# Key buffers zeroed in part by ScalarE, one-product key eviction, DMA transposes for two token blocks: a two-layer attention and mixer kernel

## The chip, the cores and the metric

The kernel runs on one core of a Trainium2 chip. A core has five engines that work at the same time, each through its own list of instructions: TensorE (PE; matrix products, results in PSUM), VectorE (DVE), ScalarE (ACT; activation functions), GpSimd (POOL) and SyncE (SP), from which this kernel issues its DMA transfers. Engines wait for each other through semaphores. The metric is the device time of one execution in microseconds (us). Before the change the median of three runs is 436.9 us (435.96 to 437.09).

## What is computed

Two layers, each an attention block A with a sliding window of 256 tokens (32 heads of 16 columns) and a mixer block B that works across tokens. There are 2048 tokens of 512 columns, in bfloat16; the same weights serve both layers. Both blocks normalise their input twice, once in the line that calls them (block B again inside).

```python
def _A_ref(x, wqkv, wo):
    B, S, D = x.shape
    H = 32; Dh = D // H; W = 256
    qkv = (x @ wqkv).reshape(B, S, 3, H, Dh).transpose(2, 0, 3, 1, 4)
    q, k, v = qkv[0], qkv[1], qkv[2]
    scores = jnp.einsum("bhqd,bhkd->bhqk", q, k) * (Dh ** -0.5)
    idx = jnp.arange(S)
    mask = (idx[:, None] - idx[None, :] >= 0) & (idx[:, None] - idx[None, :] < W)
    scores = jnp.where(mask[None, None], scores, -1e9)
    p = _softmax(scores, axis=-1)
    o = jnp.einsum("bhqk,bhkd->bhqd", p, v)
    return o.transpose(0, 2, 1, 3).reshape(B, S, D) @ wo

def _B_ref(x, w1, b1, w2, b2):
    h = _layernorm(x, axis=-1)
    u = _gelu(jnp.einsum("bsd,sf->bdf", h, w1) + b1)
    y = jnp.einsum("bdf,fs->bds", u, w2) + b2
    return y.transpose(0, 2, 1)

x = x + _A_ref(_layernorm(x, axis=-1), A_wqkv, A_wo)
x = x + _B_ref(_layernorm(x, axis=-1), B_w1, B_b1, B_w2, B_b2)
x = x + _A_ref(_layernorm(x, axis=-1), A_wqkv, A_wo)
x = x + _B_ref(_layernorm(x, axis=-1), B_w1, B_b1, B_w2, B_b2)
```

## The kernel before

**Tiling.** Tokens are cut into 16 blocks of 128 (`x_sb[:, t]`, normalised in `xh_sb[:, t]`) and into four quarters of four blocks (`m` = 0 to 3). Head columns are cut into four groups of 128 (`o` = 0 to 3), eight heads each. `prepare(m)` makes queries, keys and values of a quarter; `attention` then takes chunks of 64-token pieces (in layer 0 four or eight pieces, in layer 1 eight).

**A quarter** (`qkv`). Each block is normalised: statistics (L471, L473) on VectorE, the reciprocal root on POOL (L484), subtract and multiply on VectorE (L491). It is then transposed into `xhT`, either by TensorE against an identity (L549) with a copy out of PSUM on VectorE or ScalarE (L556, L558), or by a DMA transpose issued by SP (L542). Before the change all four blocks of quarter 0 in layer 0 go by TensorE and every other block by DMA. Quarter 0 of layer 0 is worked in two halves (columns 0 to 255, then 256 to 511), in the code the loop over `a, b` with `first` true for the first half. All matrix products of projections, the output product and the mixer's first parts go through `mm_group` (L513).

**Keys.** Scores are computed with two heads stacked in a row group of 32, so keys are kept in `kbd` with each head's columns spread to its own half and zeros in the other. In quarter 0 most keys are evicted from PSUM straight into `kbd`, by two operations that multiply with the columns of the 0/1 table `par` (L582 on ScalarE, L583 on VectorE). Other keys go through a staging tile `stg` (L594, L596) and from there by one of three ways: eight DMA copies of the rows that hold data (L604, which need the zeros written before), or two multiplications with `par` on POOL or VectorE (L609, which write the zeros too). Two memsets on POOL (L461) zero slots 1 and 2 of `kbd` at the start.

**Values.** Each pair of blocks is evicted into `vst` (L631, L633) and spread by four DMA copies into `vb` (L636).

**Attention.** Scores (L690) fill two pairs of PSUM banks; ScalarE computes the exponential into `pt` (L705); POOL or VectorE masks the diagonal pieces (L726) with the integer constants `ldm` and `ldn`, which are made at the start from a triangle `tri` on POOL (L430, L431) and six VectorE operations (L433, L435, three of L439, L454). Products with values (L747) follow, then a transpose, a reciprocal and a product (L767, L771, L773) and a second transpose (L778). Products of the next quarter and of the mixer fill TensorE's time between scores.

**The order.** Every operation is recorded as an `op` with what it reads and writes, and many with alternatives (`alts`: the same work on another engine). `ORDER` is a packed text that holds, for each place of the whole program, which operation comes next and which alternative it takes; `replay` gives each engine its list from it, and `emit` writes the semaphore waits. Each engine works in the order of its list. SP's DMAs stand in such a list too: a transfer that waits holds the ones behind it.

At the start TensorE runs 36 products on a block of ones (L392, `f_warm`), ScalarE loads its table of functions (L916), and SP issues the loads of x (L401) and of the weights (L405).

Of the kernel before, what the change touches and what calls it, by code (L numbers as in the profile page):

```python
# [7 lines left out]
dt = mybir.dt  # L8
# [7 lines left out]
    'c-qBQJ&5a87Cw^iym#m24ro9DE$D$>P@zHr1r$&~4;*kn0Tl{p!G#}q!G!|~IH1A-2lN&PwBQ9TIN-tyE*x;-!V50EV3sLdcwrV?xbVUhQ@EI7Sf+5{!o?nq'  # L16
    '$20ciz5Hx8yJyB%_g-CH-SeIAd`ALMAW$=FmRTW@UM>_MC=^Pi;EO_mPE}Ps8;@00Q*G-bFh2xcf8YPD^Jy4{4r?wJVNeNZF(i;5j)u<AALc&kTb8BtuoYXD'
    'EV9&YSZ!4!>!g`bN{ewkFV?-!CZqniE{d#Ft%9xV!b#)(TCEaPYV5=_a)q2Md&JD;Y}-<ZEX(4%qNtz|nGh-nqM(nNFd2`>41lrbFj=oV>y08w5=@sO5l;Q9'
    'E5~t`4k7c4g`?**4MwApcs`k)PYEH@>2%p2_m%ug%J;zU^<}w}Bmj_HTwbUu%%gUDrPRKHF)ZpZ8V-j>IkgT#q9zGxwOWL+*Q6H5QAD5FVugcBIS8UCVtAx5'
    'oJ<&u19$iv7cna1#_*YKJ5^OyJ|z~OtkC_q)3F@aao}aY-|XcJja+V-4ePd#=6Nr5$8=54^GwtKgfnf&d1+c%n=zA#x^CzI129br?M|l+Elo!hRD}YZf_Qqu'  # L20
    'SP)3ERD?p|W-T+p<AlWmmz&J>+$%~ixu#_`=S`xiFBAY-2B_6)1cnJql2x_3URO7ptD9B5K6*wd)Vkd{-aVgQFQ<Q>cFUdVVsW`#OsA3K%;)o&*{hi55Q9-J'
    '&$FfBG&||^{?_aDDLp%bAP7veKNy<kcP63}C9PHz{n0aH$ElgsxDhjE)LBq-b-g0Gt{ca(`sEk$b^TQ&DrE65;-xkz7100?E&w~1%|a*V<m_xVrnDCQ9!bX-'
    'm1YXX*h}M)fU!Om&@okIOl(PvC5<{j12J|S3bq}Tigu~!`;_{gMNNZdeg7q;j;bwzsGwS!B?u~0Ziq%Y!^?{V8oI8Zce{fD0`^>Em^H0dLzbj46plFn<Ww=A'
    'FQK`4LOj>DNP1RH&t|jQXq06s1sG+39kbi*t^uyE!Cc~!i-kgzrhK_Xo{tGG>%nMzHqPfML1rY`Bx!fr#C02P^EJAFZ(cjutY58xXXjs)hPF-A3lBL3pX4lJ'
    'o4RQ@9~cBgQ$#}$1OcwgE@B2$AdHBjArra3DN3SFkg5WD1k-axgz>l%2E(u)1b&%$CBINMT;FsZMb~r1oPiq~IYiJfbj!AeLw#WAgbe9`w0dBuuGqvgRI6$j'
    'Lc4<2z`#YeO+!o3Fn0_>IzT9qQcL7U7do+6@7L?yx^*Vrn%pXe80Su@MFqwhm|>=H;=0V37#a(!ArlQI2rlNJAe`WqOfhG#%;{=H-5W~sx^x5=7q*a+gflh$'
    'eZw$Pt#TZr6a%Qw`y4VQmouyne9JOS0EC7qvVzDPj44PKNl{G8B<pp1eIlAyme0J)%S%H$)eL|an)+N(`aLv4B*F~_HO#v|s2W6@$RDsi$nbjkB_tw<aCUYk'
    '2%!wcfUen!F_|78BN06ngymAB$TM;-Nt5|()|t)vvzaWn&qvv;Tm`7MhvtWaKA@`N30<K-=(ly9A_Jd|R8$)In<f)_y+1(=bS0n$TwlMwx<cq7j=u@(C`omM'
    's+WpyhcVx0`At5b6!LM*{CvrmDw0$xmkNc#rysW*%d#2dEs#FcKqmsA;wpwx&^1K`SfV3>fB;P<6ID1nqf~>FlQsVIBw?qUO$1{_QR7&{n2;j^pNrDz@KvRP'
    'TuK<mIr4oZ1y_!9SyUwYJ76btI<*!T3yU5b?QZw{9Hy=d9K2`0HxPs}^t#>t;Lp8&uVtQFrU}$Q`lqt{ZNl~Yf`ICa&~-Y75XsujO{=A87$B%rB7GV}b(9zY'  # L30
    '!{`(WoNg6MMP0AzkT0PA69N(@pXYm16Wzfq^z*(fYqEw}a{7X?cLkw<Ig%y~Rv3X&ok}t$2N6%!f^;N~$NkaC$qf0x1Uyf>-6bt(Dr%$g90?}?KF5_9Bjq&r'
    '9VRfOm7H#+>+RW`V$C>FkB<j`i7}q|K(_<XYPW`Ah;7)b*Etl+sQ&d=xDeCKb@TZ=swXnG*RcqAC>3m#2FEZ|10}nJyGwXDa!fJMLOcUE@4D;t8rCTF_KdDp'
    '|1^yA<<&pVaphmfWICUu<!>~UB*XY_G#-s?$tqjlN}AScVXSKL*K!D9S_VJ=yjH4~LRu`AgEE#cl(BpvpVe)WwLK4sNQCSM`bXp=iwJ^1G+BAkm!89|;E<#0'
    '5m!-^W`k?os-6+90>f~bsiaDi{tQqkm1!RJ6VNdN6KJ;<Xrpm^*cw#FsDIU@*6DORRU@vZyI^4JQ7JM?MU+}7R=i5t^UGK(hjfISwCi<9P;1@T^KGmPwx6?$'
    '*`}Si72oo#we1*=ty>Z<K|oE*NRs|kQo3VFj-qBWDr2RP%}Py=YhYMbK*X6DDpU<N!bV@P(lwST5xh&(i+Q7GS|c{pKw4GeK!HfSMw)Ln+D&j%-rOMigkF)W'
    'tIbAOU&8!+J`XM&6!y_r8jXS!q*_hOK?T1v(t@EBna)rd<f<%4h$aS4NQ;jOl%l*~OW_w9_o&0&&v3hj+gnZ!duhI<*Czn)Jlx^9hb0`)bV%+FN`XV$Zku+n'
    '%>ZN|?LN&sO}kq=zHOhv-X((zp6<=U-J8*Pa_H5QU5DrIHq7vcHy#^*d!K)d4tMK5e>l${9Ua~EIN<K_y7Py7!t>njX^wjX)W6uc-L~877SOvn4xM=XCjR#3'
    'ffxM4i0An?kYc;%9Wwk|$-{APJ07>ksr#_L-FWzK8n-+D0aDygj{&!b@9tr^=Pk!^+<%y7KZ6b2k1gcj|6*(}X#Cwjf54*cklzn(I)3MF&FvFM_fPP5OiFd)'
    'PDWB$dFT6#-?q>0yM*KRNS1zT!}g1NyGbT<D<hdyr!twhb1?I;1+K~*&h7>o9{)0XkL(?vf4BgDKjPoOZ+@F@{L_OaPq}pBkzPEK;jMa+EjG7q-XVq8Cxq-~'
    'fqY-CA5M)9kj(yDwjO2Pn4mw1SmuWW<UnaM{7ypdNwS?t+e|9Z`@ub6^$)5i|0od;xd4x4`DbU#p|J1k!A{$`U5U8saSyKSuRIv-&+SBsdzd5tlMLqG#I842'  # L40
    'njg9Q>mP6%x*dvl<9p-|jZg3K-1a{$!)bv|s~^WdEIxed;iHG!)%)G|$*<zszX32A5e)'
# [211 lines left out]
def mm_cost(n, cols):  # L253
    return n * (cols / 2.4 + 4.0)
# [50 lines left out]
def bass_interleave_layers__sliding_block__mixer_token_mlp__prompt_kernel(  # L305
# [29 lines left out]
    with es:  # L335
# [86 lines left out]
        for h in range(2):  # L422
# [10 lines left out]
        op("vector", lambda e: e.tensor_scalar(ldm[:, 0, :], tri[:, 0:64], half[:, 0:1], 0.0, op0=ALU.mult, op1=ALU.add),  # L433
           reads=["tri"] + HALF, writes=["ld0"])
        op("vector", lambda e: e.scalar_tensor_tensor(ldm[:, 0, :], tri[:, 64:128], half[:, 1:2], ldm[:, 0, :],  # L435
                                                      op0=ALU.mult, op1=ALU.add), reads=["tri", "ld0"] + HALF,
           writes=["ld0"])
        for i, m, c in ((1, 1.0, 0.0), (2, -1.0, 1.0), (3, -1.0, 1.0)):
            op("vector", lambda e, i=i, m=m, c=c: e.tensor_scalar(ldm[:, i, :], ldm[:, 0, :], m, c, op0=ALU.mult, op1=ALU.add),  # L439
               reads=["ld0"], writes=[f"ld{i}"])  # L440
        LD = [f"ld{i}" for i in range(4)]
# [18 lines left out]
        for k in (1, 2):  # L460
            op("gpsimd:zero", lambda e, k=k: e.memset(kbd[:, k].rearrange("p a b c d -> p (a b c d)").bitcast(dt.float32), 0.0),  # L461
               writes=["kz0"], cost=1900)
# [56 lines left out]
        def mm_group(kind, dst, n, mk, reads, cols=512, step=2, prio=None, holds=(), after=()):  # L519

            prio = fprio() if prio is None else prio
            for k0 in range(0, n, step):
                k1 = min(n, k0 + step)

                def f(e, cols32, k0=k0, k1=k1):
                    last = None
                    for k in range(k0, k1):
                        last = matmul(e, cols32, *mk(k), start=(k == 0), stop=(k == n - 1))
                    return last
                rd = reads(k0, k1) if callable(reads) else reads  # L530
                op("tensor:" + kind, f, reads=rd, writes=[dst], cost=mm_cost(k1 - k0, cols), prio=prio, holds=holds, after=after, cfg="f",
                   cls="f", flex=True)


        def qkv(m, before, split, layer):
# [3 lines left out]
            def transpose(i, wide):  # L539
# [7 lines left out]
                def f_tr(e):  # L547
# [4 lines left out]
                op("tensor:ftr", f_tr, reads=[f"xh{t}", "ident"], writes=[ft], cost=4 * 60, prio=fprio(),  # L552
                   holds=[tx], cfg="f", cls="f")
# [6 lines left out]
            def proj(o, which, a, b, wide):  # L560
# [3 lines left out]
                at = lambda: bank(ft)[:, 0:n]  # L564
                staged = m > 0 or (not layer and (o, a) in STAGED)
# [11 lines left out]
                if not staged:  # L577
                    src = lambda: at().rearrange("p (s n) -> p s n", n=64)

                    def f_ka(e, act=False):  # L580
                        for h in range(2):
                            last = (e.activation(dst(h), src(), ACTF.Copy, scale=par[:, h:h + 1]) if act else  # L582
                                    e.tensor_scalar(dst(h), src(), par[:, h:h + 1], 0.0, op0=ALU.mult, op1=ALU.add))  # L583
# [14 lines left out]
                def f_kz(e):  # L598
                    got = []
                    assert layer or m > 2 or tk.slot  # L600
# [6 lines left out]
                def f_kz2(e):  # L607
                    for h in range(2):
# [34 lines left out]
            for a, b in ((0, 256), (256, 512)) if split else ((0, 512),):  # L643
# [4 lines left out]
                for i in range(a // P, b // P):  # L648
                    transpose(i, first if m == 0 and not layer else None)
# [339 lines left out]
```

## Time and profile before

| | |
|---|---|
| median of three runs | 436.9 us |
| the profiled execution | 436.27 us |
| its span in the trace | 434.5 us |
| TensorE busy | 420.9 us (97%) |
| VectorE busy | 322.6 us (74%) |
| ScalarE busy | 317.0 us (73%) |
| POOL busy | 187.2 us (43%) |
| granted TensorE clock | 1.00 in every stretch |
| first exp (L705) | 9.40 us |
| TensorE busy in 0 to 40 us | 33.7 of 40 us |

The span is the time from the first to the last event of the trace; the device time has 1.8 us more around it. "Busy" counts an engine's instructions; matmuls are pipelined, so a TensorE that is busy throughout need not be at its peak. In the page's slices each digit is the busy share of 10.9 us in tenths. The chain of waits is followed back from the last instruction: at each step it goes to what released the waiting instruction. A line such as "L705 ACT" names the line of the kernel's text and the engine.

### The profile page before, as it was taken

Reading aid. Unit: us, or ns where it says so; the run is one execution under the profiler, and the core shown is the slowest. Engines: PE = TensorE matmul, PEld = TensorE weight load, DVE = VectorE, ACT = ScalarE, POOL = GpSimd, SP = SyncE. Lnnn points to the kernel's source line nnn. Section 1 sums busy time; section 2 is a strip of 40 time slices with the busy share of each in tenths; the row PEclk is TensorE's granted clock in tenths of the full one; section 3 lists DMA queues with packets and bytes.
Section 4 is the critical chain, followed back from the end, with each engine's and each line's share of the span. In section 5 each row is a group of like instructions: output and inputs, shape, how many; then the busy total and the mean of one; then the engine's idle time right before and its main releaser. Section 6 shows DMA issues by size and latency. Waiting matters only on the chain.

```text
span 434.5 us, 14318 instructions
## 1 busy us (share of the span) xinstructions
PE 420.9 (97%) x6177; PEld 188.5 (43%) x6177; DVE 322.6 (74%) x629; ACT 317.0 (73%) x364; POOL 187.2 (43%) x277
## 2 busy tenths in 40 slices
PE   7979989999999999999999999999999999999997
PEld 6534333434444444444444444444434444445443
DVE  7998989779996678556777999989788758422205
ACT  5999999999997953606999999899999870520000
POOL 7788865864664620011465554365435221000000
PEclk9999999999999999999999999999999999999999
DMA  8565262302163257723542282240223262747713
GB/s 237 167 125 88 63 127 37 79 5 49 26 166 83 75 152 211 208 62 88 137 110 52 64 147 64 51 77 11 47 64 99 66 175 69 226 140 213 228 32 115
DMA packets 101850, 46.03 MB, mean 106 GB/s; under 512 B 32156, under 2 KB 101788, under 8 KB 101788
## 3 DMA queue, kind: packets, MB, share of 16 engines
q1 hardware_dynamic: 101788, 45.13, 41.7%
q8 instruction: 49, 0.80, 0.8%
q14 instruction: 13, 0.11, 0.1%
HBM read 33.56 MB, written 2.10 MB: 82 GB/s over the span
## 4 chain that ended last, share of the span: by engine, by line
PE 73%; ACT 18%; DVE 6%; DMA 1%; POOL 1%; issue 0%; SPq 0%
PE PS L513 50%; ACT pt L705 17%; PE PS L868 8%; PE PS L690 8%; PE PS L747 7%; DVE stats L471 1%; DMA vb<-vst 1%; DVE xh_sb L491 1%; DVE pt L726 1%; DVE rl L767 1%; DMA x_sb<-in_A_x_dram 1%; POOL pt L726 0%; DVE stg L594 0%; DVE vst L631 0%; SPq L636 0%
## 5 line engine op out<-in xcount | busy, mean ns | idle before, releaser
L705 ACT ACTIVATE pt<-PS 128x1024 bf16<-128x1024 f32 (+1 forms) x304 | 281.0, 1036 | 13.1 <-PE PS L690 11.9
L726 POOL TENSOR_TENSOR pt<-pt,ldm 128x256 int32<-128x256 int32 (+2 forms) x189 | 125.9, 686 | 101.7 <-ACT pt L705 101.1
L513 PE MATMUL PS<-xhT,wqkv 128*128 128x512 bf16 (+1 forms) x288 | 67.8, 357 | 2.7 <-ACT pt L705 1.9
L513 PE MATMUL PS<-xh_sb,w1b 128*128 128x512 bf16 x280 | 69.9, 381 | 0.1
L513 PE MATMUL PS<-uT,w2b 128*128 128x512 bf16 (+2 forms) x308 | 68.3, 360 | 0.0
L690 PE MATMUL PS<-qT,kbd 32*128 32x64 bf16 (+4 forms) x1552 | 60.2, 247 | 3.1 <-ACT pt L705 2.1
L484 POOL TENSOR_TENSOR rstd<-agg,mhalf 128x2 f32<-128x2 f32 (+1 forms) x33 | 23.8, 722 | 66.8 <-DVE agg L473 66.7
L909 DVE SCALAR_TENSOR_TENSOR x_sb<-PS,bcol,x_sb 128x512 bf16<-128x512 f32 x31 | 22.6, 746 | 38.0 <-PE PS L513 37.7
L690 PEld LDWEIGHTS PS<-qT,kbd 32*128 32x128 bf16 x1552 | 22.7, 92 | 61.7 <-ACT pt L705 45.6
L767 DVE STREAM_TRANSPOSE rl<-PS 128x1024 f32<-128x1024 f32 x32 | 39.9, 1248 | 12.3 <-PE PS L747 12.1
L747 PE MATMUL PS<-pt,vb 64*17 64x128 bf16 (+4 forms) x3104 | 43.6, 248 | 2.4 <-DMA vb<-vst 1.1
L471 DVE BATCH_NORM_STATS2 stats<-x_sb 128x6 f32<-128x512 bf16 x64 | 44.2, 693 | 1.5 <-DMA x_sb<-in_A_x_dram 0.8
L883 ACT ACTIVATE uT<-rl,bcol 128x512 bf16<-128x512 f32 x28 | 18.3, 712 | 33.8 <-DVE rl L879 33.8
L513 PEld LDWEIGHTS PS<-uT,w2b 128*128 128x128 bf16 x308 | 27.5, 98 | 31.1 <-issue 3.2
L747 PEld LDWEIGHTS PS<-pt,vb 64*17 64x17 bf16 x3104 | 31.8, 84 | 17.6 <-issue 7.9
L513 PE MATMUL PS<-uT,pt 128*128 128x512 bf16 x168 | 39.2, 379 | 0.0
L868 PE MATMUL PS<-xh_sb,w1b 128*128 128x512 bf16 x168 | 37.7, 379 | 0.0
L513 PEld LDWEIGHTS PS<-xhT,wqkv 128*128 128x128 bf16 x288 | 24.2, 97 | 30.1 <-issue 6.3
L513 PEld LDWEIGHTS PS<-xh_sb,w1b 128*128 128x128 bf16 x280 | 23.7, 98 | 30.8 <-issue 5.9
L513 PE MATMUL PS<-wqkv,xhT 128*128 128x512 bf16 x128 | 34.2, 381 | 0.2 <-DVE stg L594 0.2
L726 DVE TENSOR_TENSOR pt<-pt,ldn 128x256 int32<-128x256 int32 (+1 forms) x77 | 29.6, 404 | 5.3 <-ACT pt L705 5.0
L513 PE MATMUL PS<-wo_sb,oT 128*128 128x512 bf16 x128 | 32.4, 380 | 0.5 <-ACT pt L705 0.5
(62 smaller groups left out, 340.7 us busy)
## 6 DMA issues: line engine op xcount, KB each, us to landing
w1b<-in_B_w_dram SPq DMA_DIRECT2D x112, 128.0 KB, 2.8
w2b<-in_B_w_dram SPq DMA_DIRECT2D x70, 128.0 KB, 2.8
pt<-in_B_w_dram SPq DMA_DIRECT2D x42, 128.0 KB, 3.0
vb<-vst SPq DMA_DIRECT2D x64, 68.0 KB, 2.1
out_dram<-x_sb SPq DMA_DIRECT2D x15, 128.0 KB, 1.8
x_sb<-in_A_x_dram SPq DMA_DIRECT2D x3, 512.0 KB, 6.2
kbd<-stg SPq DMA_DIRECT2D x80, 16.0 KB, 1.9
wqkv<-in_A_wqkv_dram SPq DMA_DIRECT2D x4, 256.0 KB, 5.4
```

What stands on the lines that cost most here:

```text
L471: op("vector:stat", lambda e: e.bn_stats(st[:, 0:6], x_sb[:, t, :]), reads=[f"x{t}"], writes=[("st", i)], cost=dve_cost(512))
L484: op("gpsimd:rstd", lambda e: e.tensor_tensor(rstd[:, t0:t1, 0], agg[:, t0:t1, 1], mhalf[:, 0:1].to_broadcast([P, t1 - t0]), op=ALU.pow), ...
L491: op("vector:xh", lambda e: e.tensor_scalar(xh_sb[:, t, :], x_sb[:, t, :], agg[:, t, 0:1], rstd[:, t, :], op0=ALU.subtract, op1=ALU.mult), ...
L513: return e.matmul(o, lhsT=w, rhs=x, start=start, stop=stop, skip_group_check=True)
L690: last = e.matmul(bank(tt[r // 2], r % 2)[:, base + c0 * 64:base + (c0 + n) * 64], lhsT=kbd[32 * r:32 * r + 32, tk.slot, o, jj].rearrange( ...
L705: op("scalar:exp", lambda e, ts=ts, tp=tp, i=i, cols=cols: e.activation(probs(tp)[:, i, 0:cols, :], pair(ts)[:, :, 0:cols].rearrange("p r ...
L726: return e.tensor_tensor(v, v, m, op=by)
L747: last = e.matmul(bank(t, h)[32 * r:32 * r + 17, i + q0 * 64:i + (q0 + n) * 64], lhsT=vb[64 * h:64 * h + 64, tk.slot, jj, 4 * o + r, :], r ...
L767: op("vector:od", lambda e, t=tod, tr=tr: e.transpose(rl[:, tr.slot:tr.slot + 2].rearrange("p a b -> p (a b)"), pair(t)), reads=[(tod, i) ...
L868: last = e.matmul(bank(tu, tt), lhsT=v()[:, sc - b0, k0 + tt * P:k0 + (tt + 1) * P], rhs=xh_sb[:, sc, :], start=(sc == b0), stop=(sc == NT ...
L883: op("scalar:gelu", lambda e, ft=ft, tt=tt: e.activation(uT[:, ft, :], rl[:, tmps[tt].slot], ACTF.Gelu_apprx_tanh, bias=b1col[:, ft:ft + 1 ...
L909: op("vector:resy", lambda e: e.scalar_tensor_tensor(x_sb[:, t, :], bank(ft), b2col[:, t:t + 1], x_sb[:, t, :], op0=ALU.add, op1=ALU.add), ...
```

## The change

- The two POOL memsets of `kbd` slots 1 and 2 (128x2048 each) become three of 128x1024 (slot 1, groups 2 and 3; slot 2, groups 0 and 1; slot 2, groups 2 and 3). Each may also be done by ScalarE, as an activation that copies a column of the identity with the scale 0. They come after the load of ScalarE's table, which is recorded earlier in layer 0. Keys of quarter 1, groups 0 and 1, lose the DMA way; only the keys that may go by DMA read the zeros.
- Five VectorE operations for `ldm` become three, of which two may go to POOL; with `ldn` that makes four.
- VectorE's direct key eviction becomes one product that reads the PSUM columns twice, against both columns of `par`. ScalarE's stays as it was.
- Blocks 2 and 3 of quarter 0 in layer 0 are transposed by DMA. Of the blocks 0 and 1, block 1's transposes are recorded first.
- Eight more products on the block of ones: two between the transposes of blocks 1 and 0, six ahead of the first key product.
- A new `ORDER`.

```diff
 ORDER = (
...
 )
...
-        def f_warm(e):
-            for _ in range(36):
-                last = e.matmul(PS[:, warm.slot, 0:P], lhsT=uT[:, 0, 0:P], rhs=uT[:, 0, 0:P], start=True, stop=True)
+        def f_warm(e, n=36, t=warm):
+            for _ in range(n):
+                last = e.matmul(PS[:, t.slot, 0:P], lhsT=uT[:, 0, 0:P], rhs=uT[:, 0, 0:P], start=True, stop=True)
             return last
         op("vector:wm", lambda e: e.memset(uT[:, 0, 0:P], 1.0), writes=["uT0"], cost=100)
+        first_tr = []
+
+        def warm_more(n, t, key):
+            op("tensor:wm2", lambda e: f_warm(e, n, t), reads=["uT0"], writes=[key], cost=56 * n, prio=fprio(), after=first_tr[-1:],
+               cfg="f", cls="f")
+
...
-        op("vector", lambda e: e.tensor_scalar(ldm[:, 0, :], tri[:, 0:64], half[:, 0:1], 0.0, op0=ALU.mult, op1=ALU.add),
-           reads=["tri"] + HALF, writes=["ld0"])
-        op("vector", lambda e: e.scalar_tensor_tensor(ldm[:, 0, :], tri[:, 64:128], half[:, 1:2], ldm[:, 0, :],
-                                                      op0=ALU.mult, op1=ALU.add), reads=["tri", "ld0"] + HALF,
-           writes=["ld0"])
-        for i, m, c in ((1, 1.0, 0.0), (2, -1.0, 1.0), (3, -1.0, 1.0)):
-            op("vector", lambda e, i=i, m=m, c=c: e.tensor_scalar(ldm[:, i, :], ldm[:, 0, :], m, c, op0=ALU.mult, op1=ALU.add),
-               reads=["ld0"], writes=[f"ld{i}"])
-        LD = [f"ld{i}" for i in range(4)]
+        def both(op_, *reads, w):
+            op("vector:ldm", op_, reads=reads, writes=[w], cost=230, alts=[("gpsimd", op_, 400)])
+        T2 = lambda h: tri[:, 64 * h:64 * h + 64].unsqueeze(1).to_broadcast([P, 2, 64])
+        both(lambda e: e.tensor_scalar(ldm[:, 0:2, :], T2(0), half[:, 0:1], 0.0, op0=ALU.mult, op1=ALU.add), "tri", *HALF, w="ld0")
+        op("vector:ldm", lambda e: e.scalar_tensor_tensor(ldm[:, 0:2, :], T2(1), half[:, 1:2], ldm[:, 0:2, :], op0=ALU.mult,
+                                                          op1=ALU.add), reads=["tri", "ld0"] + HALF, writes=["ld0"], cost=240)
+        both(lambda e: e.tensor_scalar(ldm[:, 2:4, :], ldm[:, 0:2, :], -1.0, 1.0, op0=ALU.mult, op1=ALU.add), "ld0", w="ld2")
+        LD = ["ld0", "ld2"]
...
-        for k in (1, 2):
-            op("gpsimd:zero", lambda e, k=k: e.memset(kbd[:, k].rearrange("p a b c d -> p (a b c d)").bitcast(dt.float32), 0.0),
-               writes=["kz0"], cost=1900)
+        op("scalar:tab", lambda e: e.preload_act_table_set("natural_log_exp_and_others"), writes=["acttab"], cost=1280)
+        for k, o in ((1, 2), (2, 0), (2, 2)):
+            z = lambda k=k, o=o: kbd[:, k, o:o + 2].rearrange("p a b c d -> p (a b c d)").bitcast(dt.float32)
+            op("gpsimd:zero", lambda e, z=z: e.memset(z(), 0.0), reads=["ident", "acttab"], writes=[("kz", k, o)], cost=950,
+               alts=[("scalar", lambda e, z=z: e.activation(z(), ident[:, 0:1].to_broadcast([P, 1024]), ACTF.Copy, scale=0.0), 950)])
...
+                begin = not layer and t < 2
+                if begin and first_tr:
+                    warm_more(2, ft, ft)
+                tr = op("tensor:ftr", f_tr, reads=[f"xh{t}", "ident"], writes=[ft], cost=4 * 60, prio=fprio(),
+                        holds=[tx], cfg="f", cls="f")
+                first_tr[len(first_tr):] = [tr] * begin
...
+                if wide and which and not layer and not m:
+                    warm_more(6, ft, key)
...
-                    def f_ka(e, act=False):
+                    def f_ka(e):
                         for h in range(2):
-                            last = (e.activation(dst(h), src(), ACTF.Copy, scale=par[:, h:h + 1]) if act else
-                                    e.tensor_scalar(dst(h), src(), par[:, h:h + 1], 0.0, op0=ALU.mult, op1=ALU.add))
+                            last = e.activation(dst(h), src(), ACTF.Copy, scale=par[:, h:h + 1])
                         return last
-                    two = [("vector", f_ka, 2 * dve_cost(n, psum=True, ptrs=1)),
-                           ("scalar", lambda e: f_ka(e, True), 2 * act_cost(n, 1))]
+
+                    def f_kb(e):
+                        k = [P, n // 64, 2, 64]
+                        return e.tensor_tensor(kbd[:, tk.slot, o, a // 64:b // 64], src().unsqueeze(2).to_broadcast(k),
+                                               par[:].unsqueeze(1).unsqueeze(3).to_broadcast(k), op=ALU.mult)
+                    two = [("vector", f_kb, dve_cost(2 * n, psum=True)), ("scalar", f_ka, 2 * act_cost(n, 1))]
...
+                if not layer and m == 1 and o < 2:
+                    ways = ways[:-1]
+                zeroed = [("kz", m, o - o % 2)] if not layer and m in (1, 2) and len(ways) == 3 else []
                 if not m:
                     ways = [("gpsimd", f_kz2, 1340 * n / 512)]
-                op(ways[0][0] + ":kz", ways[0][1], reads=[ts, "kz0"] + [("par", h) for h in range(2)],
+                op(ways[0][0] + ":kz", ways[0][1], reads=[ts] + zeroed + [("par", h) for h in range(2)],
...
-                for i in range(a // P, b // P):
-                    transpose(i, first if m == 0 and not layer else None)
+                for i in range(a // P, b // P)[::-1 if first and not layer else 1]:
+                    transpose(i, True if first and not layer else None)
...
-            op("scalar:tab", lambda e: e.preload_act_table_set("natural_log_exp_and_others"), writes=["acttab"], cost=1280)
+            if layer:
+                op("scalar:tab", lambda e: e.preload_act_table_set("natural_log_exp_and_others"), writes=["acttab"], cost=1280)
```

More of the change, by code (lines that the diff above doesn't have):

```diff
@@ L15 @@
 ORDER = (
[L16 to L39, printed above, removed]
@@ new lines @@
+    'E=)`U<I(I;o==DK6FQttDV@z`<JF1=fjpj!JOAkP!Iua*O9VQh<S)xbEdmivP6T0GBn6Cqzc0&4ASWb;+a*nNVzMlWX)Dggh{mgGy=GN}rXWaAt5F)&W`s;8'
+    '6GFWLaa@<nXM!-Wd=C*7z5jMQIoIuh(Q!T3Xby*F(s!Kaz8~AZZ(0a^QFk20ex7r4x|4HsJ?HAr*e5K@Yr3YW0E#Tj<Rk<NT~$pwodnu=4}vI(_{npC<;3_s'
+    'VSV4HETxXKU|9<@QdO0zhgm5rD{>8YD2TNh$FpoYpjw6IIc%fMtm>uGf1<^55k)1h4Xbq}jv+1&=ZnSn!{M;eXn6CJ$;6%v&GA^*`-72g^$@0h7>;}4aM<nk'
+    'x)$zXFc=hz`mr8%Ue)Wm-e@!%UpFFMujO*NW(|K<Dkfs7eW6yW_+mB3`6FA6s_V6?us&Y~e!eM{T#Q1o5J321yFa^!*d$nOoP}lSlc&NTmP<nb`6I%OF|FT<'
@@ L42 @@
+    '-h=n9d+p5V+LqwpFco|nR~^WXtOszLz}qed`%QZ{2RE4?Y|SHs9>QEIDsx9|8MxnvQdqKZIXIKuQ)ddrJ-P4MaJuO<?S1dvW_fMIm)BL+<U#hvuD8kE&2^U%'
+    'voE1b1a7c;o0n!@zq{8;_s!&zB`IT=ol)LR`c~d=Somtx^{K_&nIv;FH!#5bQgUQ&S^aL+UA$(1yJPOQsWP{R-cR+P?~CtbM9e!(^Anq5-ZlyIPRnHO>BH=u'
+    'GjO}s%-*_JWoPcoD#Pra-2Am+m}|(HI|trvpJDD(<Ij%&1N#3fi2'
 )
@@ L530, in mm_group @@
                 rd = reads(k0, k1) if callable(reads) else reads
-                op("tensor:" + kind, f, reads=rd, writes=[dst], cost=mm_cost(k1 - k0, cols), prio=prio, holds=holds, after=after, cfg="f",
-                   cls="f", flex=True)
+                op("tensor:" + kind, f, reads=rd, writes=[dst], cost=mm_cost(k1 - k0, cols), prio=prio, holds=holds,
+                   after=after, cfg="f", cls="f", flex=True)
         def qkv(m, before, split, layer):
@@ L599, in f_kz @@
                     got = []
-                    assert layer or m > 2 or tk.slot
+                    assert layer or m > 2 or tk.slot == m
                     for h in range(2):
@@ L607, in f_kz2 @@
                 def f_kz2(e):
+                    assert layer or m > 2 or tk.slot == m
                     for h in range(2):
```

23 lines of the change are left out of this document (19 added, 4 removed).

## The prediction

> **What bounds the kernel now.** I read the busy rows of the page first, then ScalarE's share of five stretches, then the chain of waits in order of time, then single lines. The page's slices and its summed chain:
>
> ```profile
> PE   7979989999999999999999999999999999999997
> ACT  5999999999997953606999999899999870520000
> PE 73%; ACT 18%; DVE 6%; DMA 1%; POOL 1%; issue 0%; SPq 0%
> ```
>
> TensorE is full from about 120 us on, and short of full only in the first 11 slices (10.9 us each) and at a few places later. ScalarE is full from the second slice to the eleventh: in layer 0's attention it is the scarcer of the two. Its busy time by stretch (stretch, length, busy, count):
>
> ```profile
> 9.40:34.00 24.60, 24.34 (x32) 1.00 0.60 149
> 34.00:44.00 10.00, 9.29 (x11) 1.00 0.58 94
> 44.00:81.00 37.00, 36.95 (x41) 1.00 0.42 81
> 81.00:90.00 9.00, 9.00 (x10) 1.00 0.15 39
> 90.00:98.00 8.00, 7.66 (x10) 1.00 0.05 9
> ```
>
> From its first exp (9.40 us) to 98 us ScalarE idles 88.6 - 87.24 = 1.4 us. So two things shorten this stage: an earlier first exp, and work taken off ScalarE. TensorE idles 7.5 us between 8 and 120 us (112 less its busy time there), so a gain of one or two microseconds made there on ScalarE comes out as less TensorE idle, and the TensorE-bound rest moves forward by it.
>
> The chain of waits in order of time (start, length, what) shows what sets the front:
>
> ```profile
> 5.89 0.60 DVE stats L471
> 6.49 1.35 DVE ldm L433
> ...
> 8.09 0.17 DVE ldm L435
> ...
> 8.28 0.41 DVE ldm L439 x3
> ...
> 8.71 0.30 DVE ldn L454
> 9.02 0.65 DVE xh_sb L491 x2
> ...
> 9.71 0.62 PE PS L549 x8
> ...
> 14.60 2.92 ACT pt L705 x4
> 17.52 0.26 ACT qT L574
> 17.78 1.84 ACT pt L705 x2
> 19.62 0.72 ACT kbd L582 x2
> 20.34 0.92 ACT pt L705
> 21.26 0.49 ACT vst L633
> ```
>
> Mask constants (L433 to L454) stand between the statistics of blocks 2 and 3 and their normalising (L491) on VectorE; the TensorE transposes of those blocks (L549) wait for that, and the products of blocks 0 and 1 are queued behind them. From 14.60 us ScalarE is the chain, and three evictions (L574, L582, L633: 0.26 + 0.72 + 0.49 = 1.47 us) lie in it between exps. Two rows explain the 1.35 us:
>
> ```profile
> L461 POOL MEMSET kbd<- 128x2048 f32 x2 | 3.9, 1956 | 0.0
> L433 DVE TENSOR_SCALAR ldm<-tri,half 128x64 int32<-128x64 bf16 x1 | 1.4, 1427 | 0.0
> ```
>
> The second memset runs on POOL from 5.99 to 7.79 us, and L433 from 6.41 to 7.84: a 64-column operation that its neighbours of the same width (L439) do in 0.19 us ends with the memset. VectorE was held by it.
>
> **The change, part by part.**
> *Zeroing.* Two 128x2048 memsets, 2.11 + 1.80 = 3.9 us of POOL, become three of half the size; the last quarter goes because the first two key groups of quarter 1 are no longer allowed on DMA. That costs nothing: the trace has those two on POOL already (1.36 us each, at 31.42 and 47.26). ScalarE has no such operation here; bounds: the 128x1024 exp row, 1.05 us, above, and half a POOL memset, 0.9 us, below; I take 1.05, the same engine and size. ScalarE idles from the end of its table load (2.06 us) to the first copy (5.51): 3.45 us, so all three (3.15) fit with 0.3 to spare. Cost 0; if they start more than 0.3 us late, the first copy and all behind it slip by the excess, so 0 to +0.3. Freed: L433's hold, 1.43 - 0.19 = 1.24 us of VectorE, and 0.09 us before the first rstd on POOL, which waited for the first memset's end at 4.01 with its input ready at 3.92.
>
> *Mask constants.* Six VectorE operations (1.43 + 0.24 + 0.40 for three + 0.30 = 2.37 us busy) become four, two of them twice as wide. By the 0.19 to 0.30 us rows: 0.25 + 0.25 + 0.25 + 0.30 = 1.05, so 1.3 us less VectorE, 1.24 of it the hold just named. If one goes to POOL, its cost is in the cover of POOL's idle.
>
> *Blocks 2 and 3 by DMA.* Removed: eight transposes (0.62 us of TensorE, in the chain) and two VectorE copies (0.73 us). The products behind them, which began at 10.37, can follow the first scores (end about 9.35). But ScalarE is full from 9.40, so this earns only what it lets ScalarE do sooner: I count 0 to -0.5, and take 0. Added: two DMA transposes on SP's queue, in front of the constants' loads and the x and w1 loads that SP issued at 8.71 to 11.00. Rows of the 28 that exist: issue 1.2 to 2.4 us, and
>
> ```profile
> DMA to landing us min/median/max: 2.4/3.0/4.3
> ```
>
> With blocks 2 and 3 normalised at 8.3 (1.3 us earlier), the second issue at 9.6 and 3.0 to land, they are there at 12.6. Their first product begins at 15.35. Hidden, with 2.7 us of cover; without it, the second rival. The loads behind it are late by at most 4 us; the x blocks among them are first read for statistics of later quarters, which VectorE fits in between. A rule of the Trainium skill speaks against this step: the page "VectorE: DVE Perf Modes", section "The three transpose paths", gives 390 ns for a 128x128 transpose on TensorE and 1309 ns by DMA, and advises TensorE where PSUM will do. By it, eight in a row make an estimated 10.5 us, and the landing would be near 18.8 instead of 12.6. The 28 rows here, of four 128x128 each in 2.4 to 4.3 us, do not bear the figure out.
>
> *Key eviction by one product.* Two 256-wide operations (ScalarE 0.84 to 0.88 us, VectorE 0.83 to 0.88) become one 512-element product on VectorE; nearest rows: the 512-wide TENSOR_TENSOR from PSUM, 0.67 to 0.69 us (L789, L879); an operand that repeats could cost up to the 0.88 of now. I take 0.68. The first one stood on ScalarE in series with its query (7.74 to about 8.85, scores at 8.94, exp at 9.40). On VectorE, no longer held then, the two run side by side: the 16 products from 7.11 take 1.91 us, so keys are done at about 7.6 and the query at 8.1; evicted at 8.4 and, with a cast of 0.40, at 8.5, so exp at 9.0: -0.4 us; bounds 0 (VectorE not free at 7.7) and -0.7 (with the 0.09 and the 0.12 us of L423 in the chain also gone). The later one on ScalarE (19.62, 0.72 in the chain) goes to VectorE: -0.7; bounds -0.7 and 0 (if it stays).
>
> *Relief of VectorE.* It loses 1.3 (constants) + 0.73 (copies) + 3 x 0.2 (products for pairs) and takes 2 x 0.68: 1.3 us net free. That is room for a 0.69 us value eviction, now 0.49 in ScalarE's chain, and a query (0.26). Taken: -0.5; bounds 0 and -0.75.
>
> *Warm-up products.* Eight 128-column matmuls; the 36 at the start took 4.02 us, 0.11 each: two between the transposes, six in the 0.77 us in which TensorE waits for the copy (0.67). Cost 0, up to +0.2. *Table load moved, block 1 before block 0:* no row moves; 0.
>
> Sum: -0.4 - 0.7 - 0.5 = -1.6 us, with bounds -2.7 (all far ends, with -0.75 and the transposes' -0.5) and +0.5. The profiled execution took 436.27 us, 1.77 outside its span of 434.5, and would become 434.7; it lies 0.6 under the median of 436.9, which would become 435.3. Its own range 434.2 to 436.1.
>
> **The rivals.** *(1) Nothing that can be measured.* The order of all instructions is replaced and stands packed in the text, so the choice among engines can't be read. If it keeps evictions on ScalarE, or lets TensorE's groups of six products (1.40 us) stand before scores at a few more places, the 1.2 us of relief are gone and only the first exp is earlier: 436.9 - 0.4 = 436.5. For it: ScalarE's idle from 9.4 to 98 is only 1.4 us now, which is hard to repeat. Against: VectorE gains 1.3 us in the very stretch where ScalarE's evictions lie.
>
> *(2) Slower: the transposes land late.* Place: products and values of tokens 256 to 511. The 16 DMA engines are 0.99 and 1.01 busy in 4 to 12 us and 0.87 in 12 to 16. With normalising no earlier than now (9.65), an issue of 2.44 and the 6.2 us that a 512 KB x load takes to land, the second transpose lands at 18.3; with the 4.3 of the worst transpose at 16.4. It decides from about 15.0, the first use less the 0.4 gained. Mid 17.35: 2.35 us late. Scores of the second chunk, and the value scatter that TensorE already waits for (4.01 us of DMA in the chain before 32.65), slip by as much, ScalarE empties, and the relief of 1.2 is lost in the wait: 436.9 - 0.4 + 2.35 = 438.9. Against: 2.7 us of cover by the median row. By the skill's figure above, 18.8 is beyond even that bound.
>
> *(3) A larger gain.* The new order also closes later holes: TensorE idles 1.76 us in 60 to 80 us and 0.65 in 300 to 320. Two thirds of these 2.4 more: 435.3 - 1.6 = 433.7. For it: the holes are there; against: nothing in the visible edits touches them.
>
> **How the numbers follow.** Chances: forecast 0.46, (1) 0.17, (2) 0.27, (3) 0.10. About 0.3% (1.3 us: under 435.6, over 438.2) is what a measurement of this kernel can tell from no change. Faster: 0.8 of the forecast and all of (3): 0.47. Same: 0.2 of the forecast and nearly all of (1): 0.25. Slower: (2) and a little of (1): 0.28. The predicted time is the forecast's, 435.3; the range, 433.0 to 439.0, takes in (1), most of (3) and (2) up to its middle.
>
> **What would show it.** Right: no VectorE operation on mask constants over 0.4 us; zeroing on ScalarE between 2.1 and 5.5; first exp near 9.0; product evictions near 0.68 us; no L582-like pair on ScalarE between exps; blocks 2 and 3 landed before 15 us; TensorE idle to 40 us down from 6.3 by about 1.5. Wrong: the first copy on ScalarE after 5.5, TensorE waiting on the transposed tiles, ScalarE's idle from 9 to 98 us above 3, or a difference that arises only after 120 us.

## The result and the profile after

The changed kernel takes 435.90 us (median of 17 executions, 435.28 to 436.84) beside 436.95 us before (17 executions); the ratio is 0.9979, with a 95% interval of 0.9970 to 0.9989. That is 1.05 us less, a difference that 17 executions show and that lies inside the 0.3% which the prediction counted as "same". The profiled execution took 435.28 us, its span is 433.5 us.

The page's rows and summed chain of the changed kernel:

```profile
PE   8889989999999999999999999999999999999997
ACT  6999999999997853606999999899999970601000
PE 83%; ACT 15%; DVE 1%; POOL 1%; issue 0%; POOLq 0%
```

The slices look alike; VectorE's share of the chain is 1% where it was 6%, and DMA, 1% before, has gone from it. ScalarE's busy time in the five stretches of before (stretch, length, busy, count):

```profile
9.40:34.00 24.60, 24.36 (x33) 1.00 0.87 170
34.00:44.00 10.00, 9.81 (x12) 1.00 0.33 74
44.00:81.00 37.00, 36.91 (x41) 1.00 0.33 73
81.00:90.00 9.00, 8.72 (x11) 1.00 0.22 54
90.00:98.00 8.00, 8.00 (x10) 1.00 0.14 28
```

The second row has moved most: 9.29 busy of 10 us before, 9.81 now. The last two went from 9.00 to 8.72 and from 7.66 to 8.00. Over all five, ScalarE idles 0.80 us where it idled 1.36. Up to 34 us it has done the same as before. The chain in order of time:

```profile
7.10 1.91 PE PS L520 x16
9.01 0.37 PE PS L710 x12
...
9.40 1.94 ACT pt L725 x2
11.33 0.27 ACT stg L612
...
12.59 0.27 ACT qT L587
...
24.76 9.28 ACT pt L725 x10
```

The first exp (now L725) starts at 9.40 us, exactly as before: the mask constants no longer stand behind the statistics of blocks 2 and 3, and sixteen projection products stand in the chain ahead of the first scores. ScalarE evictions still lie between exps. What is new is the unbroken stretch from 24.76 to 34.04 us and on. Before, the chain went through the scatter of the values of blocks 2 and 3 there (28.60 to 32.61 us), TensorE waited 1.06 us for it, and ScalarE was then idle for 0.68 us. TensorE's and ScalarE's timelines before:

```profile
32.65 1.52 PE L747 MATMUL PS<-pt,vb 64*17 64x64 bf16 x128 [1.06 <-DMA vb<-vst]
```

```profile
34.57 55.56 ACT L705 ACTIVATE pt<-PS 128x1024 bf16<-128x1024 f32 x60 [0.68 <-PE PS L690]
```

The landing of those four transfers, before and after:

```profile
L636 SPq DMA_DIRECT2D vb<-vst x4: 602/610/620, 26.6 to 28.6; - x4
...
DMA to landing us min/median/max: 2.9/3.5/4.0
```

```profile
L656 SPq DMA_DIRECT2D vb<-vst x4: 603/614/1190, 26.3 to 28.3; - x4
...
DMA to landing us min/median/max: 2.2/2.6/2.9
```

They are issued 0.3 us earlier and land 0.9 us faster. The 512 KB load of `wo`, issued at 25.47 us before, with only a w1 load between it and them, is now issued at 19.01.

One more number belongs to the result. Each execution states the mean clock that was granted to TensorE. Of 93 executions of the kernel before that ran beside the experiments, 32 had 0.996 or less (median 437.64 us) and 61 had 0.999 or 1.000 (436.33); all 17 of the changed kernel had 1.000. By means, these 93 have 436.84 over all and 436.38 at full clock, the changed kernel 436.04: of 0.80 us, 0.46 is the absence of executions with a lowered clock and 0.34 is left between executions at full clock.

### The profile page after: what moved, and what is told of

Its sections match the earlier page's. It is cut to its first block, busy times and chain, and to the rows that moved or that the text cites. A ratio compares the mean times of both kernels' runs of the same rounds, so it can differ in the third digit from the quotient of the medians.

```text
span 433.5 us, 14319 instructions
## 1 busy us (share of the span) xinstructions
PE 421.4 (97%) x6177; PEld 188.8 (44%) x6177; DVE 315.7 (73%) x611; ACT 319.0 (74%) x366; POOL 186.3 (43%) x282
## 4 chain that ended last, share of the span: by engine, by line
PE 83%; ACT 15%; DVE 1%; POOL 1%; issue 0%; POOLq 0%
PE PS L520 57%; ACT pt L725 15%; PE PS L710 9%; PE PS L888 8%; PE PS L767 8%; DVE rl L787 0%; DVE stats L478 0%; DVE xh_sb L498 0%; POOL rstd L491 0%; PE PS L556 0%; PE PS L392 0%; DVE agg L480 0%; POOL ldm L442 0%; DVE ldm L443 0%; DVE x_sb L915 0%
## 5 line engine op out<-in xcount | busy, mean ns | idle before, releaser
L725 ACT ACTIVATE pt<-PS 128x1024 bf16<-128x1024 f32 (+1 forms) x304 | 280.8, 1043 | 10.9 <-PE PS L710 9.8
L746 POOL TENSOR_TENSOR pt<-pt,ldm 128x256 int32<-128x256 int32 (+2 forms) x195 | 128.9, 683 | 90.0 <-ACT pt L725 89.6
L520 PE MATMUL PS<-uT,w2b 128*128 128x512 bf16 (+2 forms) x308 | 69.7, 360 | 0.0
L478 DVE BATCH_NORM_STATS2 stats<-x_sb 128x6 f32<-128x512 bf16 x64 | 42.9, 683 | 0.7
L520 PE MATMUL PS<-uT,pt 128*128 128x512 bf16 x168 | 40.9, 379 | 0.0
L498 DVE TENSOR_SCALAR xh_sb<-x_sb,agg,rstd 128x512 bf16<-128x512 bf16 x64 | 25.7, 421 | 5.5 <-POOL rstd L491 5.4
```

What stands on the lines that cost most here:

```text
L478: op("vector:stat", lambda e: e.bn_stats(st[:, 0:6], x_sb[:, t, :]), reads=[f"x{t}"], writes=[("st", i)], cost=dve_cost(512))
L498: op("vector:xh", lambda e: e.tensor_scalar(xh_sb[:, t, :], x_sb[:, t, :], agg[:, t, 0:1], rstd[:, t, :], op0=ALU.subtract, op1=ALU.mult), ...
L520: return e.matmul(o, lhsT=w, rhs=x, start=start, stop=stop, skip_group_check=True)
L725: op("scalar:exp", lambda e, ts=ts, tp=tp, i=i, cols=cols: e.activation(probs(tp)[:, i, 0:cols, :], pair(ts)[:, :, 0:cols].rearrange("p r ...
L746: return e.tensor_tensor(v, v, m, op=by)
```

## The experiments

All ratios are to runs of the kernel before on the same chip. The theory after the first look: the gain comes from the scatter's landing, thus from the order of SP's list (**queue theory**). Its rival is the prediction's: VectorE's relief and the shorter front made it (**edit theory**).

| kernel | median, us | ratio to before, 95% interval |
|---|---|---|
| the change | 435.90 | 0.9979 (0.9970 to 0.9989) |
| wo_first | 436.45 | 1.0000 (0.9983 to 1.0016) |
| edits_old_order | 442.51 | 1.0133 (1.0111 to 1.0155) |
| wo_late | 437.95 | 1.0022 (1.0004 to 1.0041) |
| scores_first | 436.24 | 0.9981 (0.9964 to 0.9997) |
| edits_loads_first | 439.32 | 1.0056 (1.0037 to 1.0075) |
| new_order_to_19 | 437.64 | 1.0023 (1.0009 to 1.0037) |
| new_order_to_87 | 435.93 | 0.9983 (0.9972 to 0.9995) |
| tensor_transposes | 435.98 | 0.9987 (0.9973 to 1.0002) |
| zeroing_alone | 436.35 | 0.9994 (0.9973 to 1.0014) |
| second_key_on_vector | 435.81 | 0.9977 (0.9963 to 0.9990) |
| to_19_wo_first | 437.33 | 1.0012 (1.0000 to 1.0025) |
| to_19_tensor | 438.40 | 1.0044 (1.0029 to 1.0059) |

The median of before was 436.95 in the first and third group of four, 436.63 in the second; the 435.90 of the changed kernel comes from a run of its own, so a difference to it is taken across groups. Each kernel of an experiment ran twelve times, edits_old_order five and edits_loads_first six. Line numbers are those of each run's own kernel.

### One transfer moved, in either kernel

wo_first is the kernel before, wo_late the changed one; each moves one line of SP's list:

```diff
 SP, kernel before (wo_first)
+  x_sb ... wo_sb<-in_A_wo            (load of wo)
   xhT<-xh_sb   DMA transpose, four times
-  wo_sb<-in_A_wo
   w1b<-in_B_w1
   vb<-vst      scatter of blocks 2 and 3
```

> The kernel before, with one operation of SP's list moved: the 512 KB load of wo stands ahead of the four DMA transposes that were issued from 18.98 us, not behind them. Queue theory (the change gains because the scatter of the values of blocks 2 and 3 no longer lands behind that load): TensorE's 1.06 us wait for vb near 32 us and ScalarE's 0.68 us of idleness near 34 us go; 0.5 to 0.7 us faster than before, span near 433.9. Edit theory (VectorE's relief in the first 25 us made the gain): no difference to before beyond 0.2 us.

> The changed kernel with one operation moved: the load of wo is issued behind the w1 load at 25.29 us, right ahead of the scatter of blocks 2 and 3, as in the kernel before. Queue theory: 0.5 to 0.7 us of the 1.0 are lost, 0.3 to 0.5 us faster than before; TensorE waits for vb near 32 us by about 1 us. Edit theory: still 1.0 us faster than before.

Measured: wo_first 0.5 us below before by the medians, but with a ratio of 1.0000 and 0.17% to either side, so nothing is shown by it. In its trace TensorE no longer waits for the scatter, but it waits 0.88 us at 27.84 us for a DMA transpose, which now stands behind the load, and ScalarE idles 0.42 us there. wo_late is 2.05 us above the changed kernel; 5 of its 12 executions had a clock of 0.996, and the other seven have a median of 437.10, 1.2 us above it. Putting the load back brings the wait back. TensorE in wo_late, and the landing of the scatter there:

```profile
33.85 1.54 PE L765 MATMUL PS<-pt,vb 64*17 64x64 bf16 x128 [0.85 <-DMA vb<-vst]
```

```profile
L654 SPq DMA_DIRECT2D vb<-vst x4: 603/607/617, 27.6 to 29.5; - x4
...
DMA to landing us min/median/max: 3.6/4.1/4.6
```

With the load right ahead, the same four transfers take 3.6 to 4.6 us instead of 2.2 to 2.9. But this trace had lost time before the load could matter. Its chain, in order of time:

```profile
11.46 5.92 DMA xhT<-xh_sb
...
17.43 1.05 PE PS L518 x8
```

TensorE waits 1.02 us for the DMA transposes of blocks 2 and 3; in the changed kernel the same products begin at 15.90 us without a wait. The exp that starts at 24.76 us in the changed kernel starts here at 26.02, 1.26 us later, and the one that starts at 43.39 there, behind the scatter, starts here at 45.64, 2.25 us later. So 1.3 us of the loss in this trace arose where both kernels have the same order, and about 1.0 us at the scatter. How much of the difference between the medians is the load's stays open.

wo_first's trace shows one of its two executions at 0.996. Its front is that of the kernel before, and in this execution (437.91 us) a load of `wqkv` landed late; TensorE's busy time by stretch, its granted clock in the fifth column:

```profile
6.00:8.00 2.00, 0.90 (x8) 1.00 0.97 312
8.00:10.00 2.00, 1.53 (x10) 0.76 1.08 346
10.00:12.00 2.00, 2.00 (x25) 0.50 0.78 197
12.00:14.00 2.00, 2.00 (x26) 0.88 1.02 340
```

TensorE stood still for 0.77 and then 0.80 us, was busy for only 0.90 of 2 us, and was then granted half its clock for some 3 us. The Trainium skill, in "TensorE: Matmul & The Clock Gate" (section "What's actually happening"), states half clock after an idle window of about 3.4 us; the half agrees with the 0.50, while here TensorE had been partly busy in the microseconds ahead of it. In edits_old_order, the next experiment, TensorE stood still for 5.62 us from 9.4 us on, and its clock was 0.75, 0.50, 0.50 and 0.55 in the four stretches of 2 us from 12 us on. A late load doesn't always bring the clock down: in edits_loads_first TensorE waited 0.34 and 0.58 us for `wqkv`, and the clock stayed at 1.00.

### The edits without the new order

```diff
 SP, edits_old_order
   x_sb<-in_A_x (4 to 7)
+  xhT<-xh_sb   DMA transpose of blocks 3 and 2
   wqkv         three loads
   tri<-b1, tri<-b2, x_sb (8 to 11), w1b ...
 SP, edits_loads_first
   x_sb<-in_A_x (4 to 7)
   wqkv         three loads
+  xhT<-xh_sb   DMA transpose of blocks 3 and 2
   tri<-b1, tri<-b2, x_sb (8 to 11), w1b ...
```

> All edits of the change with the order of before: each operation that both kernels have stands where it stood and on its old engine; the three zeroings stand on ScalarE right after its table load, the mask constants on VectorE where they were. Queue theory: the load of wo is still in the way of the scatter, so within 0.3 us of before; ScalarE idles near 34 us by 0.5 or more. Edit theory: at least 0.8 of the 1.0 us of the change, 435.9 or less beside 436.9.

> As edits_old_order, but the two new DMA transposes stand on SP's list behind the last load of wqkv instead of ahead of three of them. Theory that the 5.6 us of edits_old_order are the weight loads held behind the transposes' wait (their 5.8 us of TensorE wait): that wait is gone and the time is back at 437 within 0.7. What is left beside before is what the edits alone are worth: queue theory 0 to -0.3 us, edit theory -0.8 to -1.2 us.

Both theories are wrong here: the edits in the old order cost 5.6 and 2.7 us. In edits_old_order the transposes wait for normalised blocks and hold three weight loads behind them; from the list of waits (us in total, times, longest):

```profile
PE PS L518 <- DMA wqkv<-in_A_wqkv_dram: 5.6, 1, 5.6
```

All five executions of edits_old_order had a clock of 0.996 or less, so its 5.6 us aren't the wait alone. Behind the loads, the transposes still hold what stands after them. In edits_loads_first the biases (L447, L449) are issued at 11.79 us and x of blocks 8 to 11 at 12.81; before, these two went out at 8.71 and 9.52. From its waits, and from VectorE's timeline:

```profile
PE PS L452 <- DMA tri<-in_B_b_dram: 1.6, 1, 1.6
```

```profile
18.20 0.69 DVE L476 BATCH_NORM_STATS2 stats<-x_sb 128x6 f32<-128x512 bf16 x1 [1.40 <-DMA x_sb<-in_A_x_dram]
```

TensorE stops at the transposition of the biases, VectorE at the statistics of a late x block, and each holds the evictions behind it. The new order issues that x load at 5.82 us, ahead of the transposes, and puts the biases' transposition at 21.07 us. The reading is that the DMA transposes are bearable only with an order that clears SP's list around them. It is argued from these waits: no run has the old order and the edits with TensorE's transposes.

### Where in the new order the gain lies

new_order_to_19 and new_order_to_87 have all edits, the new order for the first 130 or 560 of 2475 operations, and the old order for the rest.

> All edits; the new order for the first 130 operations (to the 12th exp, about 19 us), the old one for the rest, so the load of wo and the w1 load are issued behind the four transposes again, ahead of the scatter of blocks 2 and 3. Queue theory: no gain over before beyond 0.3 us, ScalarE idle by about 0.7 us near 34 us. Edit theory: the front is the changed kernel's, so 0.8 us or more faster than before.

> All edits; the new order for the first 560 operations (to the 84th exp, about 87 us), the old one for the rest. If the gain is made before 87 us: the changed kernel's time within 0.3 us (435.9). If the order of the later part makes a share of it (ScalarE's exps in 98 to 120 us take 0.4 us less idle): 0.4 us or more slower than the changed kernel.

With the new order to 87 us the time is the changed kernel's (435.93), so nothing that can be measured is gained later. With the new order to 19 us it is 437.64: not faster than before, as the queue theory says, but for another reason. ScalarE is not idle near 34 us; it is idle by 1.24 us at 20 to 24. The chain there:

```profile
20.31 0.13 PE PS L452
...
20.46 0.19 DVE bcol L455
20.65 0.66 DVE qT L583 x2
21.31 0.61 DVE kbd L598
...
21.97 0.42 PE PS L708 x8
```

A join of two orders lets the biases' transposition and two queries stand ahead of a key eviction on VectorE: a cost of the join. So this kernel can't price the front alone. Its traced execution (438.29 us, the second slowest of twelve) also waits at 17.07 us, for 1.16 us, for the DMA transposes of blocks 2 and 3. Two variants of it:

```diff
 to_19_wo_first: SP
+  wo_sb<-in_A_wo
   xhT<-xh_sb   DMA transpose, four times
-  wo_sb<-in_A_wo
 to_19_tensor, and tensor_transposes on the changed kernel
-                    transpose(i, True if first and not layer else None)
+                    transpose(i, first if m == 0 and not layer else None)
```

> new_order_to_19 with the load of wo moved ahead of the four transposes on SP's list, and nothing else. If that one transfer makes the difference of 1.7 us between new_order_to_19 and new_order_to_87: 436.0 to 436.5. If it makes only the 0.7 us of ScalarE's wait: 436.9. If other parts of the order between 19 and 87 us make it: 437.6 as it was.

> new_order_to_19 with blocks 2 and 3 transposed by TensorE, as in tensor_transposes. Late-landing rival: under the old order of the rest, the first products of blocks 2 and 3 follow at once and wait for the DMA transposes (landing up to 7.6 us, first product at 17.07 us), so this kernel is 0.7 to 1.2 us faster, 436.5 to 436.9. If the transposes cost nothing: 437.6 within 0.3.

> The changed kernel with blocks 2 and 3 transposed by TensorE again (behind the first scores, as before), each with a copy on VectorE; SP has no new transposes. The prediction's step (0 to -0.5 us, taken as 0): the changed kernel's time, or up to 0.5 us slower. Late-landing rival: the DMA transposes take up to 5.3 us to land and leave no cover ahead of the first product at 15.9 us, so this kernel is 0.3 us or more faster than the changed one and its times spread less.

to_19_wo_first: 437.33, only 0.3 us better, with the same wait of 1.14 us ahead of the same scores:

```profile
21.28 1.02 ACT L723 ACTIVATE pt<-PS 128x1024 bf16<-128x1024 f32 x1 [1.14 <-PE PS L708]
```

The one load is thus not the 1.7 us between the two joins. The transposes: TensorE instead of DMA makes 0.8 us more in the join (438.40) and no difference in the changed kernel (435.98 beside 435.90). By the medians, then, TensorE's transposes gain nothing in either kernel, and the late-landing rival isn't borne out. By single traces it is at times: see wo_late and new_order_to_19 above and scores_first below.

### Three terms of the prediction, one at a time

scores_first: the changed kernel with the first key eviction on VectorE, and on TensorE

```diff
   k and q products of group 0
+  first scores
   k and q products of group 1
-  first scores
```

> The changed kernel with the first key eviction on VectorE (the product, behind block 3's statistics) and the first scores ahead of the eight projection products of group 1 on TensorE. The prediction's step of 0.4 us, in its two conditions: if the eviction and TensorE's order together hold the first exp, it starts at 9.0 us instead of 9.40. Theory that a lead at the front carries to the end: 0.3 to 0.5 us faster than the changed kernel, near 435.5. Rival, that ScalarE only waits later (its 0.56 us idle ahead of the first exp moves behind it): first exp at 9.0, no gain at 34 us and none at the end.

The first exp starts at 8.85 us, 0.55 earlier, and the time is 436.24, not below 435.90. ScalarE's timeline:

```profile
8.85 1.94 ACT L723 ACTIVATE pt<-PS 128x1024 bf16<-128x1024 f32 x2 [0.51 <-PE PS L708]
...
11.71 1.08 ACT L723 ACTIVATE pt<-PS 128x512 bf16<-128x512 f32 x2 [0.65 <-PE PS L708]
```

The third exp waits 0.65 us for the scores of group 1, whose keys go through the staging tile and POOL (TensorE waits 0.71 us for POOL's L624). The lead is used up at the next thing that is late. Behind that, this execution (436.58 us, the slowest of its twelve) loses more, to the DMA transposes; TensorE's timeline:

```profile
16.93 1.05 PE L518 MATMUL PS<-xhT,wqkv 128*128 128x256 bf16 x8 [0.76 <-DMA xhT<-xh_sb]
```

second_key_on_vector: the eviction at 19.4 us takes its other alternative, and nothing is moved.

> The changed kernel with the other key eviction that still lies between exps on ScalarE (19.4 us, two operations) done by VectorE as one product, at the same place of the order. The prediction's term: ScalarE's chain is 0.7 us shorter, so 0.5 to 0.7 us faster than the changed kernel (435.3). Rival: VectorE is 96 to 100% busy between 16 and 28 us, so 0.68 us more on it delays the queries, the values of blocks 2 and 3 and the scatter by as much, and the time is the same within 0.3 us or worse.

435.81 beside 435.90: 0.1 us, below what can be told. ScalarE has lost the eviction and waits instead, since VectorE (busy 3.95 of the 4 us from 16) has the product, and two queries and another key behind it:

```profile
20.03 1.02 ACT L723 ACTIVATE pt<-PS 128x1024 bf16<-128x1024 f32 x1 [0.59 <-PE PS L708]
```

zeroing_alone: the kernel before with the zeroing edit and nothing else.

```diff
-            op("gpsimd:zero", lambda e, k=k: e.memset(kbd[:, k]...
+            op("gpsimd:zero", lambda e, z=z: e.memset(z(), 0.0), reads=["ident", "acttab"], writes=[("kz", k, o)], cost=950,
+               alts=[("scalar", ...
```

> The kernel before with the zeroing edit alone: three halves on ScalarE behind its table load, no memset on POOL, everything else in the old order. Seen in the trace: L433's 1.43 us falls to about 0.2 and blocks 2 and 3 are normalised about 1.2 us earlier. The prediction's reading (the chain through L433 is at the front, but ScalarE is full behind it): 0 to -0.4 us beside before. Theory that VectorE's hold sets the time: -1.0 or more.

The hold is gone, exactly as read from the trace of before (VectorE's timeline):

```profile
6.39 0.24 DVE L431 TENSOR_SCALAR ldm<-tri,half 128x64 int32<-128x64 bf16 x1
...
8.31 0.72 DVE L491 TENSOR_SCALAR xh_sb<-x_sb,agg,rstd 128x512 bf16<-128x512 bf16 x2
```

1.43 us became 0.24 and blocks 2 and 3 are normalised from 8.31 instead of 8.94, half of the 1.2 us expected. At the end the median is 0.6 us lower, with 0.2% to either side of a ratio of 0.9994: a gain of up to 1.2 us or none, not told apart.

One thing in this trace (435.48 us, the second fastest of twelve) bears on the queue theory. The load of `wo` stands where it stood before, yet TensorE waits less for the scatter:

```profile
31.87 1.53 PE L750 MATMUL PS<-pt,vb 64*17 64x64 bf16 x128 [0.40 <-DMA vb<-vst]
```

The four transfers are issued 0.4 us earlier (26.20 us) and land in 2.7 to 3.7 us, and ScalarE's exps run without a stop from 21.48 us to past 46 us. So the hole near 34 us can close without moving the load. Zeroing on ScalarE is a rival for the gain that the experiments don't exclude.

## Why the prediction was right or wrong

The range held and the direction was right; 435.3 forecast, 435.9 measured, a gain of 1.05 where the sum had 1.6. But the sum is not what happened. One bound also doesn't follow from the sum: -2.7 and +0.5 on 436.9 give 434.2 to 437.4, where the text has 436.1 as the upper end. Of its signs of being right, the constants, the zeroing and the product's price came out. The first exp near 9.0, no key pair on ScalarE between exps and blocks 2 and 3 before 15 us did not. TensorE's idle time to 40 us fell by 1.0 us, from 6.3 to 5.3, instead of 1.5, and the eight added products, about 0.11 us each, count in it as work. One sign of being wrong appeared: the first copy on ScalarE began at 5.71 us, not by 5.5; it waited for TensorE's transposes, the zeroing was over.

- **Zeroing on ScalarE: right.** Three operations of 0.98 us each from 2.16 to 5.11 us, done 0.6 us before the first copy. The hold of VectorE by the memset was read rightly, and zeroing_alone shows it.
- **Mask constants: right in size.** VectorE has 0.35 + 0.28 us of them, POOL 0.67; none is over 0.4 us.
- **Key product: right in price, wrong in use.** 0.65 to 0.69 us, forecast 0.68. But the eviction at 7.74 us and the one at 19.36 us stayed on ScalarE. The term of 0.4 us for the first exp failed twice: the order did not make it, and TensorE's sixteen products ahead of the scores, which the trace of before showed (7.11 to 9.02), hold it as well. scores_first removes both and gains nothing at the end, in a trace that also waits for the transposes.
- **The later eviction, -0.7: mis-sized.** Moved, it changes the median by 0.1 us, which can't be told from nothing. Its cover was miscounted: VectorE's net room was computed over the whole front, but in the 4 us from 16 it is busy for 3.97 already, so work off ScalarE became a wait of ScalarE.
- **Relief of VectorE, -0.5: did not arise.** Before 24 us ScalarE still does a staged key, two queries, a key pair and a value block between exps; its exps up to 34 us are no further than before.
- **DMA transposes at nothing: right by the medians, with the wrong sum behind it.** The landing was mis-sized: 3.0 us were taken, the median of 28 rows, and the two took 4.7 and 5.3. They were issued at 9.16 and 10.5 us, the second was there at about 15.8 where 12.6 was forecast, and the first product began at 15.90: of 2.7 us of cover, 0.1 was left. That it held in this trace is luck. In the traces of wo_late, scores_first and new_order_to_19, TensorE waited 0.76 to 1.16 us for them. The sentence that the x blocks behind them "are first read for statistics of later quarters, which VectorE fits in between" failed in the old order: in edits_loads_first VectorE waits 1.40 us for such a block, in a kernel that is 2.7 us slower. The new order issues that load ahead of the transposes.
- **The gain itself** is not shown to lie in any of the sum's terms. The 4.01 us of the scatter stood in the chain of before, was named under the second rival, and was not priced. Setting the load of `wo` back (wo_late) loses more than the whole gain, but more than half of the loss in its trace arose ahead of the scatter; moving it forward alone (wo_first) is not told from nothing; and zeroing alone narrows the same wait in its trace. That TensorE's clock no longer drops accounts for about half of the gain by means, and was not foreseen.
- **The rivals.** The second's mechanism, late transposes, did not come about in the changed kernel's trace, but it did in the three just named: landing at about 16.9 to 17.4 us, inside the 16.4 to 18.3 that this rival worked out. It cost less than the 2.35 us foreseen, 0.76 to 1.16 of waiting, and does not show in the medians. The first rival's condition, evictions that stay on ScalarE, holds, and its outcome, a change of less than 0.3%, is the nearest by the forecast's own bound.

The cause of the gain stays open. Not settled are which part of the new order between 19 and 87 us carries it, and how much of it is the load of `wo`; what zeroing alone is worth; how often the DMA transposes land late; and what keeps the clock up. The changed kernel, scores_first, new_order_to_87, tensor_transposes and second_key_on_vector had a full clock in all 65 executions. The eight added warm-up products were not taken out in any run; they can't be all of it, since wo_late has them too.

## What to carry to other kernels

Before counting an eviction's time as gained by moving it, look at the receiving engine in the very microseconds where it lands, and at the next operand that the freed engine needs: here a lead of 0.55 us at the front ended at the next late thing. A DMA that waits on an in-order list holds what stands behind it, so order the ready loads ahead of it. A large load issued just ahead of a small transfer went with a longer landing here; try such loads where nothing waits. Price a landing by rows under the same load, not by the median of all. And a trace is one execution: see where its time lies among the others before explaining a kernel by it.

## What the hardware showed beside

The same small transfers (four of 68 KB) landed in 2.2 to 2.9 us in the changed kernel, and with a 512 KB load shortly ahead in 2.7 to 3.7 (zeroing_alone), 2.9 to 4.0 (before) and 3.6 to 4.6 us (wo_late). A DMA transpose of one block took 2.4 to 4.3 us in the kernel before. The two of blocks 2 and 3 took 2.4 and 2.5 us in edits_old_order, where three weight loads were not yet issued and the DMA engines' busy share was 0.01 in 8 to 10 us; they took 4.7 and 5.3 in the changed kernel and up to 7.7 in wo_late, behind those loads. The rule of the Trainium skill ("VectorE: DVE Perf Modes", section "Rules for kernel authors") that prefers TensorE is not borne out by the totals here: no difference in the changed kernel, 0.8 us in favour of DMA in the join. And of the 93 executions before, the 32 with a lowered mean clock were about 1.3 us longer by the median; in the traced execution of wo_first, also at 0.996, a weight load landed late and TensorE's clock was then at 0.50 for about 3 us.
